# Gated attention and hash routing on one core: another start, other engines for evictions and sorting, an early drain

## The chip, the cores and the metric

One NeuronCore of a Trainium2 chip runs the kernel. Its engines are TensorE (PE in the profile, with its weight loads as PEld), VectorE (DVE), ScalarE (ACT), GpSimd (POOL) and SyncE (SP), which here only issues DMAs. The metric is the device time of one execution in microseconds; it is the median of the runs shown. Smaller is better.

## The reference

The input is `u` and `v` of 8 x 2496 x 256, `z` of 8 x 2496 x 64, 19968 token ids, and eight experts' weights `w1` (256 x 1024) and `w2` (1024 x 256), all float32 but for the ids.

```python
scores = (1.0 / S) * np.matmul(z, z.transpose(0, 2, 1))
attn = np.maximum(scores, 0.0) ** 2
x = (u * np.matmul(attn, v)).reshape(B * S, D)
expert_idx = token_ids * np.int64(2654435761) % np.int64(E)
for e in range(E):
    mask = expert_idx == e
    h = np.maximum(x[mask] @ w1[e], 0.0)
    out[mask] = h @ w2[e]
```

Scores are symmetric, since both sides of the product are `z`.

## The kernel before, in words

The kernel has two halves. In the first, each of 8 batches is cut into 20 tiles of keys (19 of 128 rows and one of 64, which stands in twice) and 5 groups of 4 tiles of queries. A pair (batch, group) is called a run here; there are 40.

`load_z` brings z of batch 0 in with two copies of every row side by side, from SyncE's and ScalarE's queue (L121 to L126), and `turn_z` transposes it on TensorE into PSUM, from where ScalarE copies it to `zT` (L156 to L159). For later batches z is turned by VectorE (L154). The two copies are there so that `zT` holds the 64 features in both halves of the partitions: two score products with 64 rows each then run side by side.

`scores` makes the score tiles of a run (L200). Because of the symmetry a run makes only those tiles that no earlier run of the batch has made: 20 in group 0, then 16, 12, 8 and 4. Each is emptied from PSUM with the maximum with zero by ScalarE (L208), or in some places by VectorE (L206): every second tile in the very first run, and every eighth tile in groups 0 and 1 of each batch. `square` squares it on ScalarE (L222). The rest is got from earlier runs: `turns_of` and `own_turns` transpose made tiles in 32 x 32 blocks on VectorE into mirrors (L236, L252). The rooms for made tiles come from `apool`, which has 7; a room is taken again only when its turns are done. PSUM has six buffers `mm_ps`, which scores, transposes and count products share, and two accumulators `acc_ps`.

The order on each engine is written out by hand (`manual_schedule`). The loop over runs calls, step by step: `attend` (products of a made or mirrored tile with v, L325, L317 for the short tile, L297 for the short queries), `square(2)`, `turn_scores(1)` and `between()`. `turn_scores` is a budget: each step adds 1300 (first two runs) or 1600 to `turned`, and turns leave the queue `to_turn`, each costing its elements per partition plus 170, until the budget is used up. `turn_now` forces those turns which an `attend` needs at once. Near the end of a run the scores of the next one are emitted, then the last three tiles of keys in two halves, and behind each half the `gate`s: VectorE multiplies an accumulator with u (L334), which also frees it. Between the two halves stands one `turn_scores(1)`:

```python
for q in (2 * k, 2 * k + 1):
    gate(b, g, q, acc)
square(2)
turn_scores(1)
between()
```

The last group of a batch has only three whole query tiles, so its second half has one gate. While it runs, z of the next batch is turned at every second tile of keys (L607).

`between` takes one step of `places` in each of the first 40 steps (the first two runs). `places` sorts the tokens by expert: expert ids and a mask on VectorE (L401 to L405), counts by TensorE (L418) copied out of PSUM by VectorE (L419), a running sum (L422), rank by an add and a subtraction (L425, L427), small sums, and at the end an add, a multiplication and a reduction (L486 to L491) to a slot per token. Later steps scatter, from GpSimd: each token's number to its slot (L507), and each gated row of x to its slot in DRAM (L519).

In the second half (`run`, L706), blocks of 256 sorted rows go through one expert's two products: `up` (L675, emptied by ScalarE L681 and VectorE L683) and `down` (L688, emptied by ScalarE L695), and GpSimd scatters the rows of the result (L700). Before the last two blocks a value is read into registers and a branch is taken on it (L727, L730), for inputs that need more blocks; with these inputs its body is passed over. Behind it stand twelve stores for that case (L737), then the last two blocks. L764 in the profile stands for the end of the program: each engine drains, and all meet.

Of the kernel before, what the change touches and what calls it, by code (L numbers as in the profile page):

```python
# [10 lines left out]
F32 = mybir.dt.float32  # L11
# [13 lines left out]
def kernel(  # L25
# [10 lines left out]
    nc = tc.nc  # L36

    B, S, D = u.shape
    K = z.shape[-1]
    N = B * S  # L40
    E, _, F = moe_w1.shape
# [3 lines left out]
    P = 128  # L45
    TM = S // P
# [38 lines left out]


    short = const.tile([P, T, R], F32)
    nc.gpsimd.memset(short[R:P, TM, :], 0.0)
    odd = const.tile([R, D], F32)
    ident = const.tile([P, P], F32)  # L90
    make_identity(nc, ident[:])

# [6 lines left out]
    def tiles_io(dram, b, tiles, sb, store, eng, twice=False):  # L101

        rows = dram[ds(b * S, S), :]
        whole = [t for t in tiles if t < TM]
        pairs = []
        if whole:
            n = len(whole)
            pairs.append((rows[0:SM, :].rearrange("(p t) d -> p t d", t=TM)[:, ds(whole[0], n), :], sb[:, 0:n, :]))
        if TM in tiles:
            for i in range(2 if twice else 1):  # L110
                pairs.append((rows[SM:S, :], sb[ds(i * R, R), len(whole), :]))
        for d, s in pairs:
            eng.dma_start(out=d if store else s, in_=s if store else d)
# [6 lines left out]

    def load_z(b):  # L121
        if b == 0:
            zn[b] = npool.tile([P, T, 2, K], F32, name="zn")
            for i in range(2):
                tiles_io(zf, b, range(T), zn[b][:, :, i, :], False, nc.scalar if i else nc.sync, twice=True)
            return  # L126
        zn[b] = npool.tile([P, T, NQ, Q], F32, name="zn")
        rows = zf[ds(b * S, S), :]
        for q in range(NQ):
            cols = ts(q % 2, Q)  # L130
            o = zn[b][ts(q, Q)]
            for t, m in ((slice(0, TM), rows[0:SM, cols].rearrange("(j i t) k -> i t j k", i=Q, t=TM)),
                         (TM, rows[SM:S, cols].rearrange("(j i) k -> i j k", i=Q))):
                if t == TM:
                    for h in range(2):
                        nc.sync.dma_start(o[:, TM, ds(h * R // Q, R // Q), :], m)
                else:
                    nc.sync.dma_start(o[:, t], m)

    def load_v(b):  # L140
        v_sb[b] = vpool.tile([P, T, D], F32, name="v_sb")
        for g in range(NG):
            tiles_io(vf, b, group(g), v_sb[b][:, g * G:, :], False, nc.sync, twice=True)
# [5 lines left out]
    def turn_z(b, g):  # L149
        if g == 0:  # L150
            zT[b] = zpool.tile([P, T * P], F32, name="zT")
        o = zT[b][:, ts(g, G * P)]
        if b:
            nc.vector.transpose(o, zn[b][:, ts(g, G)].rearrange("p t j k -> p (t j k)"))  # L154
            return
        ps = mm_ps.tile([P, G * P], F32, name="z_ps", tag="mm")  # L156
        for i, t in enumerate(group(g)):
            nc.tensor.transpose(ps[:, ts(i, P)], zn[b][:, t].rearrange("p h k -> p (h k)"), ident[:])
        nc.scalar.copy(o, ps[:])  # L159

    def whole(g):

# [30 lines left out]
    def scores(b, g):  # L193

        n = sum(width(t) for t in group(g))
        for k, t in enumerate(fresh(b, g)):
            lo = skipped(b, g, t)
            h = ds((t % 2 if t % G < 2 else 1 - t % 2) * K, K)
            ps = mm_ps.tile([P, G * P], F32, name="s_ps", tag="mm")
            nc.tensor.matmul(ps[:, lo:n], zT[b][h, ts(t, P)], zT[b][h, ds(g * G * P + lo, n - lo)], start=True, stop=True)  # L200
            if t % G == 0:
                made[b, g, t // G] = apool.tile([P, G, G * P], F32, name="a", tag="a")
                rooms.append((b, g, t // G))
            a = made[b, g, t // G][:, t % G, lo:n]
            if k % 2 if (b, g) == (0, 0) else k % 8 == 7 and g < 2:
                nc.vector.tensor_scalar_max(a, ps[:, lo:n], 0.0)  # L206
            else:
                nc.scalar.activation(a, ps[:, lo:n], AF.Relu)  # L208
            to_square.append((b, g, t))
            if (b, g, k) == (0, 0, T // 2):  # L210
                square(EARLY)
# [58 lines left out]
    def turn_scores(steps):  # L270

        nonlocal turned

        turned += steps * (1600 if i >= 2 * T else 1300)
        while to_turn and turned > 0:
            n, _, f = to_turn.pop(0)
            f()
            turned -= n + 170
        turned = min(turned, 0)
# [70 lines left out]
    token = const.tile([P, B, T], I32)  # L350

    tok = const.tile([P, B, T, 2], I32)
    zero = const.tile([P, D], F32)
    nc.gpsimd.memset(zero[:], 0.0)
    CLEAR = T // 2
    assert NS % CLEAR == 0

# [5 lines left out]
    def load_tokens():  # L363
        tok_h = dataclasses.replace(moe_token_ids.tensor, shape=list(moe_token_ids.tensor.shape))
        tok_w = tok_h.bitcast(I32).rearrange("(b s two) -> b s two", b=B, two=2)
        nc.scalar.dma_start(tok[:, :, 0:TM, :], tok_w[:, 0:SM, :].rearrange("b (p t) two -> p b t two", t=TM))
        nc.scalar.dma_start(tok[0:R, :, TM, :], tok_w[:, SM:S, :].rearrange("b p two -> p b two"))

    def places():

        with tc.tile_pool(name="route", bufs=1) as route:
# [42 lines left out]
            for e in range(0, E, H):  # L414
                m = min(H, E - e)
                for w, dst in ((all1, total), (below, rank)):
                    ps = mm_ps.tile([P, H, C], F32, name="cnt_ps", tag="mm")
                    nc.tensor.matmul(ps[:, 0:m, :], w[:], mask[:, e:e + m, :], start=True, stop=True)  # L418
                    nc.vector.tensor_copy(dst[:, e:e + m, :], ps[:, 0:m, :])  # L419
                    yield  # L420
            flat = "p e c -> p (e c)"
            nc.vector.tensor_tensor_scan(upto.rearrange(flat), ones[:, 0:1].to_broadcast([P, E * C]), total.rearrange(flat), 0.0,  # L422
                                         op0=OP.mult, op1=OP.add)
            yield
            nc.vector.tensor_add(rank, rank, upto)  # L425
            yield
            nc.vector.tensor_sub(rank, rank, total)  # L427
            yield


# [52 lines left out]
            yield  # L483


            nc.vector.tensor_add(rank, rank, shift[:].unsqueeze(2).to_broadcast([P, E, C]))  # L486
            yield
            nc.vector.tensor_mul(rank, rank, mask)
            yield
            slot = route.tile([P, C], F32)  # L490
            nc.vector.tensor_reduce(slot[:], rank.rearrange("p e c -> p c e"), axis=AX.X, op=OP.add)  # L491
            yield
# [23 lines left out]
    def place_x():  # L516
# [5 lines left out]
        tc.declare_no_dep(st.ins, group="x", reason="each token has its own slot")  # L522
        tc.add_to_no_dep_group("x", st.ins)

    order = tc.manual_schedule()
    order.__enter__()

    load_z(0)
    load_v(0)
    load_u(0, 0)  # L530
    load_tokens()
    for g in range(NG):
        turn_z(0, g)

# [52 lines left out]
    for n, (b, g) in enumerate(groups):  # L589
# [14 lines left out]
            turn_scores(1)  # L604
            between()
        for t in range(EARLY, TM - LATE):
            if g == NG - 1 and b + 1 < B and t % 2 == 0 and t // 2 <= NG:  # L607
                turn_z(b + 1, t // 2 - 1)
            if n + 1 == len(groups) and t == T // 4:

                w_buf = list(mirrors)
                w_buf.extend(mirror[b, a, g] for a in range(NG - 1))
                load_w(0, 0)
            if n + 1 == len(groups) and t == T // 2:
                assert not gated
                x_all = vpool.tile([P, T, D], F32, name="v_sb")
                x_bufs = [x_all[:, ts(k, DP * BLK // D), :].rearrange("p c d -> p (c d)") for k in range(2 * LOADS)]
                xg_buf = [x.rearrange("p (k d) -> p k d", d=D // NQ) for x in x_bufs[:LOADS]]
                xT_buf = [x.rearrange("p (k h i) -> p k h i", h=DP, i=Q) for x in x_bufs[LOADS:]]
                for k in range(AHEAD):  # L620
                    load_x(k, k)
            if n + 1 == len(groups) and t >= TM - LATE - AHEAD:
                turn_x(t - (TM - LATE - AHEAD), t - (TM - LATE - AHEAD))
            attend(b, g, t, acc, range(G))
            if t % G == G - 1 and (b, t // G, g) in mirror and g < NG - 1:
                mirrors.append(mirror.pop((b, t // G, g)))
# [3 lines that stand above are left out]
# [17 lines left out]
        for k in range(2):  # L647
            for t in range(TM - LATE, TM):
                attend(b, g, t, acc, [2 * k, 2 * k + 1])
            for q in (2 * k, 2 * k + 1):  # L650
                gate(b, g, q, acc)
            square(2)
            turn_scores(1)
            between()
        between()
    assert not to_turn and next(place, None) is None and i > 2 * T + 4 * C
# [49 lines left out]
    def run(first, last, loads, later=None):  # L706
# [19 lines left out]
    run(0, NM, NU)  # L726
    n_used = nc.values_load(extra[0:1, 0:1], min_val=1, max_val=NB + N, engines=[  # L727
        mybir.EngineType.PE, mybir.EngineType.Activation, mybir.EngineType.DVE, mybir.EngineType.SP])
    later = []
    with tc.If(n_used > NU):  # L730
        for j in [*range(AHEAD), *range(NU, NB)]:
# [37 lines left out]
```

## Time and profile before

| | us |
|---|---|
| median of 3 runs (2670.19 to 2672.84) | 2671.82 |
| the profiled execution | 2671.7 |
| its span, first to last instruction | 2670.0 |
| first product on TensorE | 9.32 |
| first score product | 13.76 |
| first product of an attend | 22.89 |
| last store issued by GpSimd, start | 2662.99 |
| ScalarE idle for score tiles (L208), in total | 866.4 |

The page gives per engine the busy time, its share and the count of instructions. A group in the listings has the line, the engine, the operation and the tiles; behind them the busy time and the time that the engine had been idle before, with what ended it (`<-`). The timeline gives start, duration and the same, and merges instructions that follow one another (x5 is five); the duration of such a row goes from the first start to the last end. A product in float32 leaves two records on TensorE, so four query tiles of an attend are eight records. Records of products are pipelined, and their ends are modelled: the distance of two starts says more than a duration. Times are from the start of the span.

### The profile page before, as it was taken

The numbers are of one execution on the slowest core, as the hardware profiler recorded it, in microseconds if no ns is written. First come the engines' busy times: TensorE is split into PE (matmuls) and PEld (weight loads), VectorE is DVE, ScalarE is ACT, GpSimd is POOL, SyncE is SP. The second block draws the span as 40 slices with busy tenths as digits, with TensorE's granted clock in tenths as the row PEclk, the third lists the DMA queues.
The fourth block names the chain that finished last, engine by engine and source line by source line (L and its number), as shares of the span: only waits on it lengthen the run. The fifth ranks groups of instructions, "written<-read, shape, count | busy, mean of one in ns | idle before, by whom it ended". The sixth has DMA issues, their size and how long they took to land. (4 is left out here: it accounts for less than half of the span.)

```text
span 2670.0 us, 33997 instructions
## 1 busy us (share of the span) xinstructions
PE 2646.5 (99%) x12570; PEld 2250.0 (84%) x12570; DVE 1403.6 (53%) x2927; ACT 591.0 (22%) x1282; POOL 486.9 (18%) x513
## 2 busy tenths in 40 slices
PE   8999999999999999999999999999999999999998
PEld 6887888888888888888878888888888888888887
DVE  6987887878878878878869711111111111111110
ACT  4215214223233133133142111111111111111111
POOL 0122122212221222222100121111111111111113
PEclk9999999999999999999999999999999999999999
DMA  8712112202210221112101287777787777787773
GB/s 285 219 32 71 36 32 70 51 18 70 51 66 21 51 70 37 36 64 52 33 17 30 67 209 190 191 187 185 193 193 191 188 188 186 193 195 190 190 186 95
DMA packets 334843, 308.93 MB, mean 116 GB/s; under 512 B 187308, under 2 KB 293693, under 8 KB 334672
## 3 DMA queue, kind: packets, MB, share of 16 engines
q1 hardware_dynamic: 309424, 264.78, 39.7%
q0 software_dynamic: 21072, 41.10, 5.4%
q8 instruction: 101, 1.65, 0.3%
q10 hardware_dynamic: 4176, 0.82, 0.2%
q14 instruction: 70, 0.57, 0.1%
HBM read 243.25 MB, written 65.70 MB: 116 GB/s over the span
## 5 line engine op out<-in xcount | busy, mean ns | idle before, releaser
L236 DVE STREAM_TRANSPOSE m<-a 32x512 f32<-32x512 f32 (+1 forms) x1280 | 865.0, 676 | 20.7 <-ACT a L222 0.9
L325 PE MATMUL acc<-v_sb,a 128*128 128x256 f32 x3472 | 768.3, 381 | 2.2 <-DVE x_sb L334 2.2
L325 PEld LDWEIGHTS acc<-v_sb,a 128*128 128x128 f32 x3472 | 656.5, 190 | 102.4 <-issue 6.9
L683 DVE TENSOR_SCALAR hT<-h_ps 128x512 f32<-128x512 f32 x162 | 112.1, 692 | 949.5 <-PE h_ps L675 949.5
L675 PE MATMUL h_ps<-v_sb,m 128*128 128x256 f32 x2592 | 585.3, 379 | 1.5 <-ACTq L730 1.5
L688 PE MATMUL o_ps<-m,hT 128*128 128x256 f32 x2592 | 585.2, 379 | 0.0
L675 PEld LDWEIGHTS h_ps<-v_sb,m 128*128 128x128 f32 x2592 | 492.4, 190 | 68.8 <-ACTq L730 1.9
L688 PEld LDWEIGHTS o_ps<-m,hT 128*128 128x128 f32 x2592 | 492.5, 190 | 67.0
L325 PE MATMUL acc<-v_sb,m 128*128 128x256 f32 x2304 | 502.8, 379 | 0.8 <-DVE m L236 0.8
L325 PEld LDWEIGHTS acc<-v_sb,m 128*128 128x128 f32 x2304 | 437.7, 190 | 60.7 <-DVE m L236 1.2
L208 ACT ACTIVATE a<-s_ps 128x512 f32<-128x512 f32 (+2 forms) x440 | 199.5, 574 | 867.2 <-PE s_ps L200 866.4
L519 POOL DMA_INDIRECT x_rows<-x_sb,slot_i x160 | 155.2, 970 | 1070.7 <-DVE x_sb L334 894.3
L700 POOL DMA_INDIRECT out_dram<-o_sb,idx x158 | 153.5, 972 | 917.2 <-ACT o_sb L695 902.1
L222 ACT ACTIVATE a<-a 128x512 f32<-128x512 f32 (+3 forms) x472 | 231.8, 623 | 0.0
L252 DVE STREAM_TRANSPOSE a<-a 32x128 f32<-32x128 f32 (+1 forms) x992 | 220.6, 248 | 8.4
L695 ACT COPY o_sb<-o_ps 128x256 f32<-128x256 f32 x162 | 60.3, 372 | 743.5 <-PE o_ps L688 738.9
L200 PE MATMUL s_ps<-zT 64*128 64x512 f32 (+1 forms) x960 | 194.9, 545 | 1.9 <-DVE a L206 1.9
L507 POOL DMA_INDIRECT slot_tokens<-token,addr x160 | 155.2, 970 | 157.9 <-DVE addr L501 107.6
L200 PEld LDWEIGHTS s_ps<-zT 64*128 64x128 f32 x960 | 117.8, 187 | 75.0 <-issue 44.7
L681 ACT ACTIVATE hT<-h_ps 128x512 f32<-128x512 f32 x162 | 96.9, 598 | 224.9 <-PE h_ps L675 224.9
L334 DVE SCALAR_TENSOR_TENSOR x_sb<-acc,u_sb 128x256 f32<-128x256 f32 x152 | 57.8, 420 | 142.2 <-PE acc L325 141.1
L206 DVE TENSOR_SCALAR a<-s_ps 128x512 f32<-128x512 f32 (+1 forms) x40 | 25.8, 645 | 91.4 <-PE s_ps L200 91.4
(77 smaller groups left out, 318.5 us busy)
## 6 DMA issues: line engine op xcount, KB each, us to landing
m<-in_moe_w_dram SPq DMA_DIRECT2D x324, 256.0 KB, 6.6
m<-in_moe_w_dram SPq DMA_DIRECT2D x81, 1024.0 KB, 6.3
x_rows<-zero SPq DMA_DIRECT2D x10, 2176.0 KB, 18.2
v_sb<-x_rows SPq DMA_DIRECT2D x324, 64.0 KB, 6.2
v_sb<-in_v_dram SPq DMA_DIRECT2D x32, 512.0 KB, 5.2
u_sb<-in_u_dram SPq DMA_DIRECT2D x32, 512.0 KB, 3.9
zn<-in_z_dram SPq DMA_DIRECT2D x28, 304.0 KB, 4.5
v_sb<-in_v_dram SPq DMA_DIRECT2D x8, 384.0 KB, 8.9
```

The costliest lines, as they stand in the source:

```text
L200: nc.tensor.matmul(ps[:, lo:n], zT[b][h, ts(t, P)], zT[b][h, ds(g * G * P + lo, n - lo)], start=True, stop=True)
L208: nc.scalar.activation(a, ps[:, lo:n], AF.Relu)
L222: nc.scalar.square(o, x)
L236: nc.vector.transpose(mirror[b, a, g][ts(c, Q)].rearrange("p t s q -> p (t s) q")[:, 0:m, ts(r, Q)], made[b, a, g][ts(r, Q)].rearrange("p ...
L252: return n * Q, lambda: nc.vector.transpose(out, in_)
L325: nc.tensor.matmul(acc[i // 2][:, i % 2, :], lhs(b, g, t, i), v_sb[b][:, t, :], start=(k == 0 and i % 2 == 0), stop=(k == TM - 1), skip_gr ...
L507: st = nc.gpsimd.indirect_dma_start(out=slot_dram[:, None], out_offset=bass.IndirectOffsetOnAxis(ap=addr[0:n, c:c + 1], axis=0), in_=token ...
L519: st = nc.gpsimd.indirect_dma_start(out=x_dram[:, :], out_offset=bass.IndirectOffsetOnAxis(ap=slot_i[0:width(c % T), c:c + 1], axis=0), in ...
L675: nc.tensor.matmul(ps[:, i, :], w1[j][:, c, ts(f + i, P)], xT[j][:, :, c, :], start=(c == 0), stop=(c == DP - 1))
L683: nc.vector.tensor_scalar_max(o, ps[:], 0.0)
L688: nc.tensor.matmul(ps[:], hT[j][:, f, ts(t, P)], w2[j][:, f, :], start=(f == 0), stop=(f == FP - 1))
L700: st = nc.gpsimd.indirect_dma_start(out=out[:], out_offset=bass.IndirectOffsetOnAxis(ap=rows, axis=0), in_=o, in_offset=None, bounds_check ...
```

## The change

It has these parts.

- z of batch 0 is loaded once, one piece of 19 x 64 numbers per partition, in a tile with one more column block; VectorE copies the last block to the first. A transpose takes two neighbouring blocks, so the lower half of its result belongs to the tile before. VectorE copies the upper half to `zT`, ScalarE the lower half, shifted by a tile; one more small copy follows.
- GpSimd clears `zero` first. ScalarE copies one number, and TensorE multiplies `zero` with itself six times, ahead of z. The tokens' DMAs go from ScalarE's to SyncE's queue, ahead of u.
- In group 1 of every batch ScalarE alone empties the scores. (In group 0 the eighth tiles stay with VectorE.)
- The budget of the first two runs is 1450 a step; the step between the gates adds 0.8 of a step.
- z of the next batch is turned four tiles of keys later.
- ScalarE copies the counts, both of a step at once; two adds, a subtraction and a multiplication of the sort go to GpSimd, with three more empty steps ahead of the reduction.
- GpSimd drains ahead of the branch.

```diff
@@ load_z
-            zn[b] = npool.tile([P, T, 2, K], F32, name="zn")
-            for i in range(2):
-                tiles_io(zf, b, range(T), zn[b][:, :, i, :], False, nc.scalar if i else nc.sync, twice=True)
+            zn[b] = npool.tile([P, T + 1, K], F32, name="zn")
+            tiles_io(zf, b, range(T), zn[b][:, 1:, :], False, nc.sync, twice=True)
+            nc.vector.tensor_copy(zn[b][:, 0, :], zn[b][:, T, :])
@@ turn_z
-            nc.tensor.transpose(ps[:, ts(i, P)], zn[b][:, t].rearrange("p h k -> p (h k)"), ident[:])
-        nc.scalar.copy(o, ps[:])
+            nc.tensor.transpose(ps[:, ts(i, P)], zn[b][:, t:t + 2].rearrange("p t k -> p (t k)"), ident[:])
+        nc.vector.tensor_copy(o[K:P], ps[K:P, :])
+        i = 0 if g else 1
+        nc.scalar.copy(zT[b][0:K, ds((g * G + i - 1) * P, (G - i) * P)], ps[0:K, i * P:])
+        return ps
@@ scores
-            if k % 2 if (b, g) == (0, 0) else k % 8 == 7 and g < 2:
+            if k % 2 if (b, g) == (0, 0) else k % 8 == 7 and g == 0:
@@ turn_scores
-        turned += steps * (1600 if i >= 2 * T else 1300)
+        turned += steps * (1600 if i >= 2 * T else 1450)
@@ places
-                    nc.vector.tensor_copy(dst[:, e:e + m, :], ps[:, 0:m, :])
-                    yield
+                    nc.scalar.copy(dst[:, e:e + m, :], ps[:, 0:m, :])
+                yield
...
-            nc.vector.tensor_add(rank, rank, upto)
+            nc.gpsimd.tensor_add(rank, rank, upto)
             yield
-            nc.vector.tensor_sub(rank, rank, total)
+            nc.gpsimd.tensor_sub(rank, rank, total)
...
-            nc.vector.tensor_add(rank, rank, shift[:].unsqueeze(2).to_broadcast([P, E, C]))
+            nc.gpsimd.tensor_add(rank, rank, shift[:].unsqueeze(2).to_broadcast([P, E, C]))
             yield
-            nc.vector.tensor_mul(rank, rank, mask)
-            yield
+            nc.gpsimd.tensor_mul(rank, rank, mask)
+            for _ in range(4):
+                yield
@@ the start
+    WARM = 6
+    nc.scalar.copy(odd[0:1, 0:1], zero[0:1, 0:1])
+    warm = mm_ps.tile([P, D], F32, name="warm", tag="mm")
+    for _ in range(WARM):
+        nc.tensor.matmul(warm[:], zero[:, 0:P], zero[:], start=True, stop=True)
     load_z(0)
     load_v(0)
+    load_tokens()
     load_u(0, 0)
-    load_tokens()
-    for g in range(NG):
-        turn_z(0, g)
+    z_ps = [turn_z(0, g) for g in range(NG)]
+    nc.scalar.copy(zT[0][0:K, ts(TM, P)], z_ps[0][0:K, 0:P])
@@ the loop over runs
-            if g == NG - 1 and b + 1 < B and t % 2 == 0 and t // 2 <= NG:
-                turn_z(b + 1, t // 2 - 1)
+            if g == NG - 1 and b + 1 < B and t % 2 == 0 and t // 2 > 2:
+                turn_z(b + 1, t // 2 - 3)
...
-            turn_scores(1)
+            turn_scores(1 if k else 0.8)
@@ ahead of the branch
+    nc.gpsimd.drain()
     later = []
     with tc.If(n_used > NU):
```

## The prediction

> **What bounds the kernel now.** I read the page first, to see which engine the end hangs on:
>
> ```profile
> span 2670.0 us, 33997 instructions
> PE 2646.5 (99%) x12570; PEld 2250.0 (84%) x12570; DVE 1403.6 (53%) x2927; ACT 591.0 (22%) x1282; POOL 486.9 (18%) x513
> ```
>
> TensorE is busy 99% of the span: work taken off another engine counts only where TensorE waits for it. None of its products is removed, so everything there is to win lies in its waits, in stretches at a slow clock, and in the time ahead of its first and behind its last product. So, second, TensorE's waits (line, releaser: us in total, times, longest):
>
> ```profile
> PE z_ps L158 <- DMA zn<-in_z_dram: 9.3, 1, 9.3
> PE acc L325 <- DVE x_sb L334: 2.2, 7, 0.3
> PE s_ps L200 <- DVE a L206: 1.9, 1, 1.9
> PE h_ps L675 <- ACTq L730: 1.5, 1, 1.5
> PE acc L325 <- DVE m L236: 0.8, 1, 0.8
> ```
>
> The list reckons with modelled ends, so a product drawn out over a wait hides part of it; I size each from starts. Third, the timeline at the two VectorE waits. The first, at 60 us, is in the second run (batch 0, query group 1):
>
> ```profile
> 59.37 0.71 DVE L236 STREAM_TRANSPOSE m<-a 32x512 f32<-32x512 f32 x1
> 60.10 0.69 DVE L206 TENSOR_SCALAR a<-s_ps 128x512 f32<-128x512 f32 x1
> 60.17 0.60 ACT L208 ACTIVATE a<-s_ps 128x512 f32<-128x512 f32 x1 [0.84 <-DVE m L236]
> 60.85 0.31 PEld L200 LDWEIGHTS s_ps<-zT 64*128 64x128 f32 x4 [2.74 <-DVE a L206]
> 60.85 2.38 PE L200 MATMUL s_ps<-zT 64*128 64x512 f32 x6 [1.91 <-DVE a L206]
> ```
>
> VectorE has fallen behind with turning and sorting; TensorE stands for PSUM, and ScalarE (second-last idle) for a room that VectorE has not finished turning. The windows (us, busy and count of PE, PEld, DVE, ACT, POOL, clock, DMA, GB/s) show the after-effect, a clock of 0.87 instead of 1.00:
>
> ```profile
> 52.70:66.00 13.30, 11.39 (x43) 5.91 (x40) 9.97 (x14) 9.42 (x19) 0.00 (x0) 0.87 0.30 98
> ```
>
> The other comes seven times, where a batch ends:
>
> ```profile
> 598.61 0.76 DVE L334 SCALAR_TENSOR_TENSOR x_sb<-acc,u_sb 128x256 f32<-128x256 f32 x2 [3.39 <-PE acc L325]
> 599.28 2.12 DVE L236 STREAM_TRANSPOSE m<-a 32x512 f32<-32x512 f32 x3
> 601.43 0.42 DVE L334 SCALAR_TENSOR_TENSOR x_sb<-acc,u_sb 128x256 f32<-128x256 f32 x1
> 601.91 1.35 PE L325 MATMUL acc<-v_sb,a 128*128 128x256 f32 x5 [0.32 <-DVE x_sb L334]
> ```
>
> Three turns sit between the two gates; the third gate ends at 601.85 and frees the accumulator at which TensorE resumes. Last, the closing instructions (ns min/median/max):
>
> ```profile
> L764 POOLq DRAIN  x3: 40/108/6433, 2662.8 to 2669.7; - x3
> L764 SPq DRAIN  x3: 7/7/13, 2666.3 to 2669.4; - x3
> ```
>
> SyncE is through with all its DMA waits at 2666.4; GpSimd's drain runs from 2662.75 to 2669.18 and holds everyone.
>
> **Start: z, warm-up, copies.** In before z is 1.2 MB (each row stored twice) in 256 B pieces; in that stretch the DMA listing shows some 216 GB/s, and about 400 GB/s once the 4 KB pieces of v and u flow. Now 0.6 MB goes once, in runs of 4.9 KB: 1.6 us at 400 GB/s. From the first packet at 2.3 it ends at 3.9; plus 1.1 to the waiter (last z packet 8.2, TensorE 9.32): 5.0. A VectorE copy of 64 columns (0.17 to 0.24 by the small copies) and handovers: 5.4. The warm-up: zero, now cleared first, is there at 0.82+0.32, TensorE starts near 1.2; six products are twelve records of 256 columns, 0.2155 apart at full clock and twice that at half: 5.1 us, until 6.3. So the warm-up ends last, not z. All twenty transposes stand ahead of the first score. They came 0.213 apart; at full clock at best 0.107: over at 8.4 to 10.6. The zT copies are split, and the order shows a new wait: each ScalarE half waits for VectorE's half of the same PSUM tile. Four transposes done at 7.0, two VectorE copies at 0.69 (L206, 512 columns) and one of ScalarE at 0.59 with handovers: 9.2. Scores start at 9.3, against 13.76. The next ones follow these copies 0.69 apart, so the first six take 2.5 us; in before 2.6, the first pair being slow. Gain 4.4.
>
> Here a rule matters: TensorE: Matmul & The Clock Gate (Part 1) says that the full clock comes after about one busy window of 3.4 us. The row: TensorE starts at 9.32, and score pairs reach their later pace at about 14.6, 5.2 us on. By the row the clock is up at 6.4, by the rule between 4.6 and 8.1; with 8.1 some transposes are slow and scores begin at 9.4. If it stays down until all are through, 10.7. Ends: 5.4 (z and clock early) and 2.6 (z lands 2 us later than the warm-up). The table load and the tokens' two DMAs, now on SyncE behind v and ahead of u, cost nothing: tokens are first used at 26.12, u at 67.3, and 2.6 MB of v takes under 7 us.
>
> **Second run.** From the first score of run (0,1) to that of (0,2) is 45.61 us; in batches 1 to 7 the same run takes 40.51. Batch 0 computes 2 x 256 columns more of scores, 0.2. So 4.9 is lost there: wait and slow clock together. Does it go? ScalarE alone takes 0.50 a tile (eleven in 5.50 at 53.82) against TensorE's 0.43; after 16 tiles it is 1.1 us behind, and six PSUM buffers cover 2.6. What is late next is the room: tile 12 of the run needs all 32 early turns. Laid end to end in before's time: VectorE starts at 24.67; 32 turns at 0.71 are 22.8, remaining sorting 5.5 (two small pairs 0.9, mask 1.5, scan 2.9, two crumbs 0.2): 53. Needed at 53.82+12x0.50 = 59.8. Cover 6.8 us. Gain 4.9, ends 4.0 and 5.1. In the other seven runs VectorE loses two evictions each and ScalarE, idle 866 us for scores, takes them: nothing.
>
> **Sorting moved.** Six PSUM copies (L419, 3.4 us) go to ScalarE. Queued behind their waits are four squares; their tiles are attended at least seven steps later, over 10 us. Two adds, a subtraction and a multiplication of 128x1280 (1.49 each) go to GpSimd, which has nothing else until its first scatter. GPSIMD Engine Reference (4.1 Engine selection) speaks against it: two-input elementwise work is about twice as slow there; from its 4497 ns for 2048 elements I estimate 2.8 us. No run of before has such a row; the nearest is GpSimd's memset, 4.37 us for 5120 elements, or 1.1 for 1280. By either, the last pair has 33 turns (over 20 us) of cover before VectorE's reduction asks for it. SBUF — State Buffer (two separate sides) adds that such an operation can lock VectorE out. Even 4x2.8 = 11.2 us of standing, against 6.0+3.4 removed, leaves VectorE 1.8 worse; the part ahead of the room is 5.6, inside 6.8. I take 0. The mask comes one turn later (11 turns ahead of it, not 10): counted from 34.31 against the count product at 35.09, a loss of 0.1 (0 to 0.3).
>
> **Turns.** 1450 instead of 1300 in the first two runs, and the time VectorE wins, put it several turns ahead. Run (0,4) takes 33.22 against 32.12 later: 1.1 us lost to turns at 196.65 and 206.5. z's turns move four steps later there, so two of them (1.4) leave the queue ahead of the late turn: gain 1.1 (0.4 to 1.1). In later batches the last zT turn has 5.6 us of cover and the last own turn 3.9; nothing VectorE does there waits for TensorE, and the total work is the same: 0. Between the gates that end a batch the order now shows two turns for three. The gate ends 0.71 earlier, at 601.1; TensorE, 0.48 late (start to start 0.70 instead of 0.2155), is freed: 7x0.48 = 3.4 (3.0 to 3.4).
>
> **Early drain.** It stands on GpSimd ahead of the twelve stores that follow the branch. The three drains with nothing outstanding took 0.04 to 0.19; the long one ended 5.2 us after the last scatter was issued (2663.96) and about 4.2 after its last packet (2665.0). If this is bookkeeping over everything issued since the start, the early drain takes most of it, and the end then hangs on SyncE: 2669.23-2666.43 = 2.8. If it is a fixed price of any drain after a scatter, 0. Nothing in the trace separates these; the landing having long passed, I lean to the first: 2.8. Its price: 5.2 us ahead of 15 stores at 1.28, queued from 2634.7. They end at 2659.1, before the last store at 2663.0 needs GpSimd: hidden, with 3.9 us left.
>
> **Sum.** 4.4+4.9+1.1+3.4-0.1+2.8 = 16.5. The profiled execution took 2671.7 (span 2670.0 and 1.7 around it), the runs' median is 2671.8: 2655.2.
>
> **Rivals.** (1) The drain is a fixed price: 13.7, 2658.0. For it: a 17-store backlog must be drained anyway. (2) The start gives only 2.6, z landing late, and the drain nothing: 11.9, 2659.8. (3) The VectorE stall does not go but shifts: sorting on GpSimd locks VectorE out for more than the 6.8 us of cover, and the 4.9 stays: 2660.1 with the drain's gain, 2663 without. Against: it takes 4 us and more for each operation before the room. (4) Slower than before: the early drain walks all 489 or so scatters at a price that grows. The last store needs GpSimd at 2663.0, so a drain above 9.1 us pushes the end one for one; above 9.1+13.7 = 22.8 us it eats every gain, and at 30 us the time is 2679. Against: the one at the end took 5.2 with the same count. (5) The change doesn't do what it says: long pieces land no earlier than 9.3, because what is slow there is the first DMA and not its pieces; start gain 0, 2659.6. Against: once packets flow, the rate follows the piece size (216 to 400 GB/s).
>
> **Chances.** Forecast 0.50, (1) 0.26, (2) and (5) 0.12, (3) 0.08 (half of it within 0.2%), (4) and other new waits 0.04. About 0.2%, 5.3 us, is what the measurement can tell from no change. Faster by more 0.92, within 0.05, slower 0.03. Range: all upper ends, 5.4+5.1+1.1+3.4+2.8 = 17.8, give 2654, and a microsecond for what I have not seen makes 2653; the high end takes in (1), (2) and (5), 2661.
>
> **What would show it.** First score near 9.3 and first attend near 18.5 (22.89 now); no PE wait on an eviction or at 196, interval (0,1) to (0,2) near 40.7; no wait for x_sb at the seven batch ends, each batch 189.5 instead of 190.0; a long drain near 2620 and a short one at the end, the end 0.8 us after SyncE's drain. I am wrong if z lands after 7, if GpSimd's sums take over 4 us, or if the last drain keeps its 5.2.

## The result and the profile after

The changed kernel takes 2655.82 us (median of 6 runs, 2654.62 to 2656.08), the kernel before, run beside it, 2672.19 (6 runs): ratio 0.9939, interval 0.9926 to 0.9951. The prediction said 2655.2, in a range of 2653 to 2661. The profiled execution took 2655.88, its span is 2654.2; before it was 2670.0, so 15.8 us have to be accounted for.

From the page, the span and the engines' busy time:

```profile
span 2654.2 us, 34028 instructions
PE 2646.6 (100%) x12582; PEld 2254.3 (85%) x12582; DVE 1391.6 (52%) x2907; ACT 599.4 (23%) x1306; POOL 500.8 (19%) x517
```

TensorE's busy time is the same to 0.1 us with twelve records more (the warm-up). All that was won is time in which TensorE did nothing or ran slowly. Its waits (line, releaser: us in total, times, longest), complete:

```profile
PE warm L540 <- POOL zero L90: 1.2, 1, 1.2
PE h_ps L688 <- ACTq L745: 1.1, 1, 1.1
PE s_ps L208 <- ACT zT L166: 0.3, 1, 0.3
```

The waits for z, for the eviction (`a L206`), for a mirror (`m L236`) and the seven for `x_sb` are gone; the one at the branch stays. The start, in the timeline (start, us, engine, operation):

```profile
1.18 5.42 PE L540 MATMUL warm<-zero 128*128 128x256 f32 x12 [1.18 <-POOL zero L90]
...
6.37 0.20 DVE L128 COPY zn<-zn 128x64 f32<-128x64 f32 x1 [6.37 <-DMA zn<-in_z_dram]
...
6.66 2.37 PE L163 MATMUL z_ps<-ident,zn 128*128 128x128 f32 x20
...
9.30 9.20 PE L208 MATMUL s_ps<-zT 64*128 64x512 f32 x40 [0.26 <-ACT zT L166]
```

z is there at 6.37 and VectorE's copy of it over at 6.57, the warm-up ends at about 6.5, twenty transposes take 2.4 us, so some 0.11 each and not the 0.213 of before, and the first score comes at 9.30. The end of batch 2 (batches are counted from 0), around its gates:

```profile
584.89 5.45 PE L333 MATMUL acc<-v_sb,a 128*128 128x256 f32 x24
...
587.79 0.75 DVE L342 SCALAR_TENSOR_TENSOR x_sb<-acc,u_sb 128x256 f32<-128x256 f32 x2 [3.38 <-PE acc L333]
588.46 1.41 DVE L244 STREAM_TRANSPOSE m<-a 32x512 f32<-32x512 f32 x2
...
589.90 0.42 DVE L342 SCALAR_TENSOR_TENSOR x_sb<-acc,u_sb 128x256 f32<-128x256 f32 x1
```

Two turns stand between the gates, where it was three; the third gate is over at 590.3, and TensorE goes on without a wait. The early drain (L743) and the closing ones (L779; ns min/median/max, then first and last start in us):

```profile
L743 POOLq DRAIN  x1: 5132/5132/5132, 2620.7 to 2620.7; - x1
L779 POOLq DRAIN  x3: 46/108/3297, 2649.7 to 2653.9; - x3
L779 SPq DRAIN  x3: 7/7/13, 2653.3 to 2653.6; - x3
```

GpSimd's long one is over at 2653.0, before SyncE's at 2653.3; before, GpSimd came 2.75 us after SyncE.

The account, by starts of TensorE's products. "(b,g)" is the time from the first score of run (b,g) to that of the next run.

| | before | after | won | forecast |
|---|---|---|---|---|
| first attend product | 22.89 | 18.43 | 4.46 | 4.4 |
| (0,1) | 45.61 | 41.14 | 4.47 | 4.9, less 0.1 |
| (0,4) | 33.22 | 32.12 | 1.10 | 1.1 |
| (b,0), b = 1 to 7 | 41.93 | 41.35 | 7 x 0.58 | 7 x 0.48 |
| (b,1), b = 1 to 7 | 40.51 | 40.71 | -7 x 0.20 | 0 |
| gap at the branch | 1.86 | 1.51 | 0.35 | 0 |
| start of the last product's last record to the end | 8.07 | 5.33 | 2.74 | 2.8 |
| sum | | | 15.8 | 16.5 |

### The profile page after: what moved, and what is told of

It is laid out like the page before. It is cut to its first block, busy times and chain, and to the rows that moved or that the text cites. A ratio compares the mean times of both kernels' runs of the same rounds, so it can differ in the third digit from the quotient of the medians.

```text
span 2654.2 us, 34028 instructions
## 1 busy us (share of the span) xinstructions
PE 2646.6 (100%) x12582; PEld 2254.3 (85%) x12582; DVE 1391.6 (52%) x2907; ACT 599.4 (23%) x1306; POOL 500.8 (19%) x517
## 4 chain that ended last, share of the span: by engine, by line
PE 57%; issue 35%; POOL 6%; POOLq 0%; DMA 0%; DVE 0%; ACT 0%
PE acc L333 47%; PE s_ps L208 7%; POOL out_dram L713 6%; PE acc L325 2%; PE q_ps L305 1%; POOLq L713 0%; PE warm L540 0%; POOL v_sb L677 0%; DMA out_dram<-v_sb,idx 0%; POOL x_rows L526 0%; DVE zT L164 0%; POOLq L779 0%; POOLq L743 0%; PE cnt_ps L424 0%; PE z_ps L163 0%
## 5 line engine op out<-in xcount | busy, mean ns | idle before, releaser
L216 ACT ACTIVATE a<-s_ps 128x512 f32<-128x512 f32 (+3 forms) x456 | 205.4, 588 | 845.6 <-PE s_ps L208 845.5
L595 DVE STREAM_TRANSPOSE v_sb<-v_sb 128x512 f32<-128x512 f32 x81 | 56.7, 700 | 0.0
```

## The experiments

In every profile of an experiment run (0,2) takes 40.4 to 41.4 us (42.8 once) where both profiles behind the result have 38.58, and some have 1 to 2 us more in the last blocks; the kernel before, run beside them, took 2675.4 to 2677.1 us (medians) and not 2672.2. So times are compared with the kernel before in the same group of runs, and parts by their own intervals. Four kernels ran once only, beside one run of before at 2677.08: without warm-up 2661.39, with z's odd rows first 2662.13, with z's turns early 2659.52, with three drains 2660.59. Their times settle nothing, and only their intervals are read. More on this stall at the end.

**Without the early drain.**

```diff
-    nc.gpsimd.drain()
     later = []
```

> The changed kernel without the early drain. Theory A (the drain at the end has to work through what was scattered since the last drain): the last drain is again some 5.2 us past the last scatter, as before the change, and the span grows by 2.7 us to 2656.9. Rival B (the last drain is shorter for another reason, say the other order at the start, and the early one does nothing): 2654.2, and the last drain stays at 3.3 us. A side question: TensorE's wait at the branch fell from 1.86 to 1.51 us start to start; if the drain did that, it is 1.86 again here, otherwise 1.51.

2660.97 us, ratio 0.9945 (0.9928 to 0.9961). From the last product's start to the end it takes 8.1 us, 2.7 more than with the drain. The closing drains:

```profile
L778 POOLq DRAIN  x3: 40/108/6438, 2652.9 to 2659.9; - x3
L778 SPq DRAIN  x3: 7/7/13, 2656.6 to 2659.6; - x3
```

The last GpSimd drain takes 6.44 us as it did before (6.43), and SyncE is again done 2.8 us ahead of it. The drain is worth its 2.7; a fixed price of each drain is out. The gap at the branch was 2.00 here, and with the drain in place 1.58 and 1.84 in the next two kernels. Over all profiles it is 1.34 to 2.04 with the drain and 1.85 to 2.00 in the three without, so nothing shows that the 0.35 in the account is the drain's.

**VectorE again empties an eighth of group 1's tiles; sorting stays moved.**

```diff
-            if k % 2 if (b, g) == (0, 0) else k % 8 == 7 and g == 0:
+            if k % 2 if (b, g) == (0, 0) else k % 8 == 7 and g < 2:
```

> The changed kernel with every eighth score tile of group 1 given back to VectorE. Theory A (with the sorting moved, VectorE has time, and ScalarE alone is too slow by 0.2 us in each of the seven later runs): interval (b,1) to (b,2) back from 40.71 to 40.51 in batches 1 to 7, the span 1.4 us shorter, near 2652.8, with (0,1) still near 41. Rival B (ScalarE alone is what cures the second run): (0,1) goes back towards 45.6, and the span is 3 us longer, near 2657.

2657.93 us, ratio 0.9932 (0.9916 to 0.9949). (0,1) takes 40.94 and (b,1) 40.51. With VectorE, run (2,1) looks like this:

```profile
430.02 6.61 PE L208 MATMUL s_ps<-zT 64*128 64x512 f32 x32
...
431.08 6.75 ACT L216 ACTIVATE a<-s_ps 128x512 f32<-128x512 f32 x14 [22.49 <-PE s_ps L208]
...
433.70 0.69 DVE L214 TENSOR_SCALAR a<-s_ps 128x512 f32<-128x512 f32 x1 [2.18 <-PE s_ps L208]
```

and with ScalarE alone, in the changed kernel:

```profile
427.96 6.81 PE L208 MATMUL s_ps<-zT 64*128 64x512 f32 x32
...
429.01 7.52 ACT L216 ACTIVATE a<-s_ps 128x512 f32<-128x512 f32 x16 [22.48 <-PE s_ps L208]
...
433.62 0.19 PEld L208 LDWEIGHTS s_ps<-zT 64*128 64x128 f32 x1 [0.24 <-ACT a L216]
```

The 16 tiles take TensorE 0.20 us more when ScalarE must empty all of them. So this part of the change costs 0.2 in each of eight runs, and it is not needed against the stall of (0,1): with the sorting moved, the bigger budget and the earlier start, (0,1) is even 0.2 shorter without it.

**A full step between the gates again.**

```diff
-            turn_scores(1 if k else 0.8)
+            turn_scores(1)
```

> The changed kernel with a full step of turns between the gates. Theory A (the third turn stands before the gate that frees the accumulator): the wait of 0.48 us comes back at the seven ends of a batch, with 0.1 us behind each, and the span grows by 3.4 to 4.1 us to about 2658. Rival B (VectorE is so far ahead in the changed kernel that the gate is in time anyway): 2654.2.

2663.21 us, ratio 0.9955 (0.9939 to 0.9972). (b,0) is back at 41.94, seven gaps of 0.70 are back. The end of batch 2:

```profile
590.65 0.76 DVE L342 SCALAR_TENSOR_TENSOR x_sb<-acc,u_sb 128x256 f32<-128x256 f32 x2 [3.39 <-PE acc L333]
591.32 2.12 DVE L244 STREAM_TRANSPOSE m<-a 32x512 f32<-32x512 f32 x3
...
593.48 0.42 DVE L342 SCALAR_TENSOR_TENSOR x_sb<-acc,u_sb 128x256 f32<-128x256 f32 x1
...
593.95 2.21 PE L333 MATMUL acc<-v_sb,a 128*128 128x256 f32 x9 [0.32 <-issue]
```

Three turns, the third gate over at 593.90, TensorE on at 593.95. The wait has "issue" as its name here (idle time for which the trace names no releaser) and a releaser in before; the gap between the starts is the same. The part is worth 7 x 0.58 = 4.1.

**Before, with the eviction change alone.**

```diff
-            if k % 2 if (b, g) == (0, 0) else k % 8 == 7 and g < 2:
+            if k % 2 if (b, g) == (0, 0) else k % 8 == 7 and g == 0:
```

> The kernel before, with only group 1 emptied by ScalarE alone. Theory A (VectorE is late in the second run through sorting, and without its eviction ScalarE still waits for the room that VectorE turns at 60.1): ScalarE stands under 1 us, TensorE hardly, so the interval (0,1) falls from 45.6 to between 40.9 and 42.5; batches 1 to 7 lose 0.2 each; in all 2 to 3 us shorter than 2670.0. Rival B (the sorting has to move as well): (0,1) stays above 44, and the span is 2670 to 2671.

2671.62 us, ratio 0.9986 (0.9979 to 0.9993). That is 3.8 us less than the kernel before took beside it (1.9 to 5.6), where 2 to 3 were expected. (0,1) falls from 45.61 to 41.14, just as in the changed kernel; (b,1) rises to 40.71; (0,4) keeps its 33.22. The second run:

```profile
53.20 7.24 PE L200 MATMUL s_ps<-zT 64*128 64x512 f32 x32
...
60.60 2.06 ACT L208 ACTIVATE a<-s_ps 128x512 f32<-128x512 f32 x4 [0.36 <-DVE m L236]
```

ScalarE still stands 0.36 us for the room, and TensorE goes through without the gap of 1.91 us that before has at this place: it was VectorE's eviction, queued behind its late turns, that held TensorE. Taking VectorE's two evictions away cures the second run by itself; so do the other edits without it (the second experiment), and no run tells which of the sorting, the budget and the start is needed there. The change does both, and the second remedy to come is worth nothing there, or -0.2.

**No warm-up.** Leaves out the six products whose result nobody uses.

```diff
-    WARM = 6
+    WARM = 0
```

> The changed kernel without its six warm-up products at the start (their result is used by nothing). Theory A (the start gains because the clock comes up and z comes in at the same time): z is ready at about 6.6 us, as with the warm-up, but the twenty transposes then run at half clock, 0.213 apart, so that the first score comes at about 11.3 instead of 9.30, with some first scores slow too: first attend about 2.0 to 3.5 us later than 18.43. Rival B (what was won is z's alone, the warm-up gives nothing): first score at 9.3, first attend at 18.4. Rival C (the warm-up itself holds the transposes, since it ends at 6.4): transposes begin before 6.4.

First score 10.57, first attend 19.81. In the timeline:

```profile
5.85 0.19 DVE L128 COPY zn<-zn 128x64 f32<-128x64 f32 x1 [5.85 <-DMA zn<-in_z_dram]
...
6.14 4.50 PE L163 MATMUL z_ps<-ident,zn 128*128 128x128 f32 x20 [6.14 <-DVE zn L128]
...
10.57 9.31 PE L208 MATMUL s_ps<-zT 64*128 64x512 f32 x40
```

z came at 5.85, and the transposes start 0.3 later and lie 0.213 apart, twice the distance of those behind the warm-up; the full clock is granted only at 11.53. Two kernels of the same group with the warm-up and z at 5.57 and 5.91 have the first attend at 18.31 and 18.02: the warm-up is worth 1.5 to 1.8 us. With z at 6.37, as in the changed kernel's own profile, the first attend would by these rows have come at about 20.3 without it, so an estimate of 1.9 there. The expected 2.0 to 3.5, reckoned with z at 6.6, were too much. Of the 4.46 won at the start 1.5 to 1.9 is then the warm-up's, and the rest is z's.

**z's odd rows first, on ScalarE's queue** (with the eighth for VectorE as above).

```diff
-            tiles_io(zf, b, range(T), zn[b][:, 1:, :], False, nc.sync, twice=True)
+            tiles_io(zf, b, range(TM, T), zn[b][:, T:, :], False, nc.scalar, twice=True)
+            tiles_io(zf, b, range(TM), zn[b][:, 1:, :], False, nc.sync)
```

> The changed kernel with VectorE again emptying an eighth of the second run's PSUM tiles, and with z's odd rows (the last of z to land, at 6.30) loaded first and on ScalarE's queue, the main part on SyncE's. Theory A (z and the warm-up end together, and the next limit is the warm-up): z is ready before 5.8 us, transposes begin at 6.4 with the warm-up's end instead of 6.66, first score 0.1 to 0.3 us earlier than 9.30. Rival B (the two queues share what they move, nothing lands earlier): first score at 9.3. Rival C (odd rows in 256 B pieces on the other queue hold up the long pieces): first score later than 9.4. In both (0,1) takes 40.94 and (b,1) 40.51, as in the run with VectorE's eighth alone.

z came later, and with it the first score, at 10.75:

```profile
7.82 0.20 DVE L129 COPY zn<-zn 128x64 f32<-128x64 f32 x1 [7.82 <-DMA zn<-in_z_dram]
...
8.11 2.37 PE L164 MATMUL z_ps<-ident,zn 128*128 128x128 f32 x20 [1.58 <-issue]
```

Rival C. v is issued from 1.29 on here, and from 2.52, behind all of z, in the changed kernel; the odd rows' packets, issued at 1.17 and 1.76, run only from 5.05 to 7.14. That they now share the DMA engines with v is the likely reason, but was not tried by itself. Though TensorE stood 1.6 us between the warm-up and the transposes, these were at full clock (granted at 1.00 from 6.26 on).

**z's turns at their earlier steps again.**

```diff
-            if g == NG - 1 and b + 1 < B and t % 2 == 0 and t // 2 > 2:
-                turn_z(b + 1, t // 2 - 3)
+            if g == NG - 1 and b + 1 < B and t % 2 == 0 and t // 2 <= NG:
+                turn_z(b + 1, t // 2 - 1)
```

> The changed kernel with the turns of the next batch's z back at their earlier steps (even steps 2 to 10 of the last query group, not 6 to 14). Theory A (run (0,4) gains since VectorE is several turns ahead when it gets there): the run stays at 32.12 us. Rival B (it gains since z's turns come later, as the prediction has it): it goes back to about 33.2, 1.1 us up. In the other batches nothing moves in either, since the zT turns have more than 2 us of cover.

(0,4) stays at 32.12. In before TensorE waited there for VectorE's last turns into a mirror:

```profile
195.44 1.16 DVE L236 STREAM_TRANSPOSE m<-a 32x384 f32<-32x384 f32 x2
...
196.65 3.72 PE L325 MATMUL acc<-v_sb,m 128*128 128x256 f32 x16 [0.84 <-DVE m L236]
```

The last of these turns starts 22.2 us after the run's first score in before, and also with the eviction change alone; 17.1 after it here; and 15.7 in the changed kernel. So VectorE's lead, which comes from the sorting, the budget or the start, is worth 5.1 us and suffices for the 1.1; z's later turns bring the turn forward by another 1.5. Whether they would suffice alone was not tried.

**More drains.** One behind the first half's scatters, two in a row ahead of the branch:

```diff
     while gated:
         place_x()
+    nc.gpsimd.drain()
...
     nc.gpsimd.drain()
+    nc.gpsimd.drain()
     later = []
```

> The changed kernel with more drains of GpSimd: one behind the scatters of the first half of the batches (some 320 of them), and two in a row in place of the one ahead of the branch (about 158 scatters since the first). Theory A (a drain pays for the scatters issued since the last one): with the points known, 3.3 for 17 and 5.1 for 478, a drain after 320 takes about 4.5 us, one after 158 about 3.8, the second of the pair under 0.2, the last again about 3.3. Rival B (a drain pays a price that hangs on what was issued since the start): the one after 478 again takes 5.1, and so does the last but for what the one ahead saves. Rival C (a fixed price of any drain behind recent stores): both of the long ones alike. End within 0.3 us of the changed kernel's 5.37 after the last product, since all of them lie ahead of it.

and one with drains behind chosen scatters:

```diff
+    sent = [0]
+    def count(marks):
+        sent[0] += 1
+        if sent[0] in marks:
+            nc.gpsimd.drain()
...
         tc.add_to_no_dep_group("slots", st.ins)
+        count((8, 24, 56, 120))
...
         tc.add_to_no_dep_group("x", st.ins)
+        count((168, 176, 192, 224, 288))
...
         tc.add_to_no_dep_group("rows", st.ins)
+        count((336, 344, 360, 392, 456))
```

> The changed kernel with GpSimd drains behind chosen scatters: in each of the three sorts (token numbers, rows of x, rows of the output) behind 8, 16, 32 and 64 scatters since the last one, the drain ahead of the branch as it is, now 22 after the last. Known so far, us past the end of the last scatter's issue: 2.1 after 17, 4.8 after 158, 8.5 after 320, 3.9 after 478, 5.2 after 489, so the price does not rise with the count all the way. Theory D (a price for each scatter not yet cleared away, of which some are cleared in lumps between drains): it rises evenly with the distance at 0.02 to 0.12 us a scatter, alike for the three sorts, about 1.5 to 2.5 us after 8 and 3 to 8 after 64. Rival E (it hangs on what the DMA queues move at that moment): no order by distance. Rival F (a fixed price behind a recent scatter): all between 1.5 and 2.5 us. The time itself: within 2 us of the changed kernel's if TensorE never waits for one of these scatters.

Token numbers and rows of x are scattered in turn, so the marks left other distances than meant. Worked out from the trace, over both kernels, the changed one and before; "landed" is the end of the last packet of GpSimd's queue.

| scatters since the last drain | us past the last scatter's issue | us past the last packet landed |
|---|---|---|
| 0 (second of a pair) | | 0.05 long |
| 8 | 1.8 | 0.7 |
| 16 (the end, as changed) | 2.1 | 1.0 |
| 22 | 3.4 | 1.4 |
| 48 | 4.0 | 2.9 |
| 56 | 4.7 | 3.1 |
| 64 | 5.3 | 4.5 |
| 112 | 9.2 | 8.1 |
| 158 | 4.8 | 2.6 |
| 320 | 8.6 | 7.5 |
| 478 (early drain, as changed) | 3.9 | 2.7 |
| 494 (the end, before) | 5.2 | 4.2 |
| 8, 16, 32, 48, 64, among stores of the second half | 6.4, 6.3, 7.5, 7.7, 8.2 | 1.3, 2.1, 2.1, 2.8, 3.4 |

Up to 112 the price past landing rises with the distance, by 0.04 us a scatter among stores of the second half ((3.4-1.3)/56) and 0.07 elsewhere ((4.5-0.7)/56); where other transfers delay the landing, that is added. Beyond 112 it does not follow the count: 478 cost less than 64. The first of the two kernels' Theory A falls, the second's Theory D holds up to 112. What happens beyond (a clearing in between would fit the order) stays open. The kernel with eleven drains, most over 5 us, took 2658.44 in its one run, the changed kernel beside it 2658.55: GpSimd has the time. With the drains of the first kernel the end still comes 5.33 us after the start of the last product (the 5.37 expected was reckoned from rounded times).

**The changed kernel and the version with VectorE's eighth, side by side.**

> The changed kernel itself once more, as the reference beside the next one. By the earlier runs: about 0.994 of the time before, with a stall of 2 to 3 us in run (0,2) where this chip shows one in every kernel run on it so far.

> The changed kernel with VectorE again emptying an eighth of the PSUM tiles of the second query group's runs, sorting and start as changed. Theory A (ScalarE alone makes TensorE wait in each of these runs): 0.20 us less in each of eight intervals, 1.6 us less in all, ratio to the changed kernel 0.9994. Rival B (the wait moves to the room or to a later run, and nothing is left): the same time as the changed kernel. Either way the drains and the start stay as they are.

Changed: 2658.55 (2657.88 to 2658.86), ratio 0.9935 (0.9922 to 0.9949). With the eighth: 2657.32 (2656.38 to 2661.24), ratio 0.9936 (0.9922 to 0.9949). In the profiles each of the eight intervals is 0.20 shorter, 1.6 in all, and nothing else longer on account of it; the runs scatter by 1 to 5 us, so the times alone do not separate the two kernels.

## Why the prediction came out, step by step

- **The start** (4.4; measured 4.46). Right in size, by two errors that cancel. z was mis-sized: ready at 6.6, not 5.4, and so last by 0.1 to 0.2, where the forecast had the warm-up last. (In the eight other profiles with this start VectorE's copy begins at 5.5 to 5.9, and the warm-up was last in seven.) The long pieces were not what bound it: their last packet ends at 4.47, that of the odd rows, still in 256 B pieces and issued behind them, at 5.92. Transposes begin at 6.66 for 6.3, so the warm-up hid all but 0.4 of this error, and the way from them to the first score was shorter by as much (2.6 us, not 3.0). The time at which the clock comes up: the prediction took 5.2 us after TensorE's start from one row against the 3.4 of TensorE: Matmul & The Clock Gate (Part 1) in the Trainium skill. By the granted clock in the trace it came 5.2 us after in the changed kernel, and in the other twelve profiles 3.5 to 5.6, so both ends occur. That section also says that the window runs freely, so that the cold stretch varies from run to run; these rows agree, but over 2.1 us, where the section has half a microsecond either way.
- **The second run** (4.9; measured 4.47). The wait and the slow clock went, and no new one came at the room. Two terms were mis-sized. The columns that batch 0 computes more cost 0.43, not 0.2 (40.94 against 40.51 with the eighth given back), so only 4.67 was lost there. And the step "six PSUM buffers cover 2.6" failed and, from it, "nothing" for the other seven runs. The sum set ScalarE's arrears of 1.1 us after 16 tiles against the six buffers, and left out that ScalarE starts 1.05 us after TensorE (427.96 and 429.01). Both together are 2.15, still inside 2.6. What is missing fits two more things that the rows show: an eviction takes 0.6 to 0.7 us before its buffer is free, and two tiles run side by side on TensorE and so take two buffers at once. In run (2,1) ScalarE ends its ninth tile at 433.53 and its tenth at 434.02; TensorE's records due, by the pace up to there, at 433.54 and 433.97 start at 433.62 and 434.07, and the last of the 32 is 0.20 late. That is the 0.20 in each of eight runs, and 4.67 less 0.20 is the 4.47.
- **Which edit cures it.** The prediction laid VectorE's work end to end with all edits made. The runs show that the eviction change is enough alone, and so are the others without it.
- **Sorting moved** (0). Right. The four operations on GpSimd took 2.89, 2.90, 2.32 and 2.61 us, where GPSIMD Engine Reference (4.1 Engine selection) of the Trainium skill led to an estimate of 2.8 and the memset to 1.1; on VectorE they took 1.49. The rule was the better guide, and cover made it free: none of TensorE's waits names them. Of the 11.2 us for which VectorE might have stood, 0.9 are seen (last section).
- **Run (0,4)** (1.1; measured 1.10). The number is right, the reason given for it was not needed: "several turns ahead", which the prediction named first, gives 5.1 us of lead and is enough, and with z's turns put back nothing changed.
- **Gates** (7 x 0.48). The wait is gone, as forecast; another 0.10 in each (b,0) went with it. The eviction's 7 x 0.20 hid that: a batch takes 189.61, where 189.5 was forecast and the version with VectorE's eighth takes 189.41.
- **Early drain** (2.8; measured 2.7). Right that the last one becomes short and that the end then hangs on SyncE. The reason, bookkeeping over everything since the start, holds only in this: the price follows what was issued since the last drain, up to some hundred scatters. Rival (1), the fixed price, and rival (4), a price that grows with all 489, both fall.
- **Not forecast.** The gap at the branch was 0.35 shorter; over all profiles it lies between 1.3 and 2.0, and no experiment explains it.

So the sum promised 0.7 more than came, and the time was 0.6 too low. By parts: 1.4 too much at the PSUM buffers of seven runs and 0.3 in (0,1), against 0.7 at the gates and 0.35 at the branch that were not forecast. That the number came so close is then partly luck: without these two gains it would have missed by some 1.7. The reason counted at (0,4) cost nothing. Rivals (2) and (5), no or little gain at the start, fall with the first score at 9.30, and rival (3), the stall that only shifts, with (0,1) at 41.14.

## What to carry to other kernels

When an engine is relieved of evictions, count for the one that takes them its start lag and the time of one eviction, as well as its slower pace, against the buffers; the loss is small for one run and comes back in every run. Two remedies for one stall are not two gains: try each alone. A drain of GpSimd placed earlier, where nobody waits for GpSimd, can take some microseconds off the end, as long as few scatters follow it.

## What the runs showed of the hardware that was not expected

- While a GpSimd sum over 128x1280 ran, a VectorE addition of 128x8, 0.12 us long in before, took 1.01 us and ended with it, while the 32x32 transposes beside it kept their 0.71:

```profile
67.66 2.32 POOL L492 TENSOR_TENSOR zn<-zn,shift 128x1280 f32<-128x1280 f32 x1 [20.32 <-DVE shift L461]
69.00 1.01 DVE L467 TENSOR_TENSOR late<-shift,m 128x8 f32<-128x8 f32 x1
```

- A gap in TensorE's work of a few microseconds can cost more behind it: in the kernel with z's odd rows on ScalarE's queue the granted clock was 0.50 from 122.31 to 125.73, 3.41 us, 0.4 us after TensorE had gone on from the stall of run (0,2), as in before from 62.3 to 65.7, 1.4 us after its stall. The longest gaps ahead of these two stretches were 2.1 and 2.5 us between starts; in the other profiles gaps of up to 2.0 us, at the branch, left the clock at 1.00.
- That stall, at 117 to 125 us, is in all eleven experiment profiles (1.8 to 2.8 us, and 4.2 with the slow clock) and in neither profile behind the result. The trace calls it "issue"; VectorE's, ScalarE's and the DMA queues' rows around it are the same in a profile with it and one without. Its cause is open. It does not come from the change: the changed kernel itself has it in one profile (40.57) and not in another (38.58), and before with the eviction change alone has it too.
